# Attention quotients: one transfer for each head in place of one for a pair of heads

## The chip, the cores and the metric

The kernel runs on one core of one Trainium2 chip. The core has a matrix engine (TensorE, PE in the profile), a vector engine (VectorE, DVE), a scalar engine (ScalarE, ACT), a general engine (GpSimd, POOL) and SyncE (SP), which here only issues transfers; sixteen DMA engines move the data. The metric is the time of one execution on the device in microseconds (us), the median of several runs. Lower is better.

## The reference

Sixteen heads (2 batches of 8) of attention over 768 tokens with head dimension 64, where a query sees only the keys of its own cluster, and then two feed-forward parts over all 1536 tokens. The quotients of this case are the divisions by the softmax sums.

```python
mask = q_assign[:, :, :, None] == k_assign[:, :, None, :]
scores = np.where(mask, scale * np.matmul(q, k.transpose(0, 1, 3, 2)), -1e9)
scores = scores - np.max(scores, axis=-1, keepdims=True)
attn = np.exp(scores)
attn = attn / (np.sum(attn, axis=-1, keepdims=True) + 1e-09)
x = np.matmul(attn, v)                 # (2, 8, 768, 64)
x = x.transpose(0, 2, 1, 3).reshape(1536, 512)
x = ((x @ w1) * (x @ w2) @ w3) @ w_out # first feed-forward part
h = x @ w_in
out = softplus(h) @ w_out2             # second
```

## The kernel before

Attention is worked through in eight pairs of heads (`pi` 0 to 7). A pair has three blocks of 256 queries (`T`, 0 to 23 over all pairs), and a block has three slots (`o`, 0 to 71), one for each 256 keys. In a slot TensorE makes the scores (`st_pe`, L723, into the bank `sb`), ScalarE takes the exponential (`st_exp`, L730), and TensorE multiplies the slot before by V (`av_pe`, L741); after a block's third slot `sum_pe` (L751) sums the exponentials into the other half of the same bank `avb`. Every score is made of two matmuls: one over 128 rows of the operands, and one over 97 rows, whose last row is the row minimum of the block (the scores are held negated).

This minimum comes round a corner. `mx` (L671, L677) makes a block's scores ahead of time and VectorE reduces them to columns `mn`; `m_row` (L701 to L712) turns the columns into rows on TensorE (L705), ScalarE copies them to a tile `mr` (L65), and two small transfers `q<-mr` (L710, 1 KB each) put them on partition 96 of the query tile `q`. The second matmul of the block's first score reads that row.

The sums take another way, `r_ev` (L764 to L783) and `av_ev` (L756 to L762): to a DRAM buffer `sd` (L762), back as columns `r` (L771), one over the sum on VectorE (L774, L777), to a DRAM buffer `rd` of two rows of 768 numbers, one row for each head of the pair (L779), and from there to the tile `R` of 128 partitions (L783): row 0 copied to partitions 0 to 63, row 1 to partitions 64 to 127. `x_norm` (L793, GpSimd) multiplies the unscaled result by `R`.

The attention part is recorded with a fixed order: what stands first in the code stands first in its engine's queue, and each engine works its queue in order. The four steps of `r_ev` for a pair come at the ends of four slots in the first half of the next pair, the last of them being L783; the next slot begins with `m_row`, and so SyncE issues `q<-mr` right behind `R<-rd`. `x_norm` comes two slots later. Almost all transfers are issued by SyncE and go through one queue; they signal on eight semaphores in turn, so that each waits for the landing of the one eight places before it. Beside attention, TensorE works out a product of the weights w3 and w_out (L555, L574), whose weights come in loads of 512 KB (`w3r`, L93). For each next pair, SyncE loads heads (`rawqk`), and copies split queries and keys to the operand tiles (L360 to L367). After slot 72 the two feed-forward parts follow (L912, L934, L1213, L1282).

Of the kernel before, what the change touches and what calls it, by code (L numbers as in the profile page):

```python
# [27 lines left out]
def fused_kernel(ctx: ExitStack, tc, q, k, v, centroids, w1, w2, w3, wo, w_in, w_o2, out):  # L28
# [6 lines left out]
    nc = tc.nc  # L35
    B, H, S, D = q.shape
# [620 lines left out]
    MN, E, TT, R = {}, {}, {}, {}  # L657
# [106 lines left out]
    def r_ev(pi, i):  # L764

        if i == 0:
            pass
        elif i == 1:
            R["t", pi] = sp.tile([P, 8, QC], F32, tag="r", name=f"r{pi}")
            s = R.pop(("s", pi)).rearrange("r b n -> r (b n)")  # L770
            nc.sync.dma_start(R["t", pi][:, :4], s.rearrange("r (a x) -> a r x", x=QC))  # L771
        elif i == 2:
            t = R.pop(("t", pi))
            nc.vector.scalar_tensor_tensor(  # L774
                out=t[:, 4:6], in0=t[:, 0:4:2], scalar=1e-9, in1=t[:, 1:4:2], op0=ALU.add, op1=ALU.add
            )
            nc.vector.reciprocal(t[:, 6:], t[:, 4:6])  # L777
            R["d", pi] = drp.tile([2, S], F32, tag="rd", name=f"rd{pi}")
            nc.sync.dma_start(R["d", pi].rearrange("j (a x) -> a j x", x=QC), t[:, 6:])  # L779
        else:  # L780
            R[pi] = sp.tile([P, S], F32, tag="R", name=f"R{pi}", bufs=1)
            d = R.pop(("d", pi))
            nc.sync.dma_start(R[pi], d.unsqueeze(1).to_broadcast([2, D, S]))  # L783

    def x_norm(pi):
        b, c = divmod(pi, CC)
# [227 lines left out]
    with tc.manual_schedule():  # L1014
# [71 lines left out]
        for o in range(NSLOT + 1):  # L1086
# [48 lines left out]
            for pi in range(NPAIR):  # L1135
                r = a - 3 * NB * pi - 3 * NB
                if r in RS:
                    r_ev(pi, RS.index(r))
                if r == XR:
                    x_norm(pi)  # L1140
# [14 lines left out]
    for i in range(4):  # L1155
        r_ev(NPAIR - 1, i)
# [194 lines left out]
```

## Time and profile before

| what | value |
|---|---|
| median of 3 runs | 891.96 us (887.86 to 892.52) |
| the profiled execution | 889.03 us, its span 887.0 us |
| TensorE busy | 814.9 us, 92% of the span |
| VectorE, ScalarE, GpSimd busy | 439.3, 396.2 and 222.8 us |
| mean granted clock of TensorE | 0.96 |
| moved by DMA | 76.00 MB, mean 86 GB/s |

The profile is that of one execution. A wait is shown with the instruction that ended it. The chain is the work that ended last, followed back from the end: time on it is time that the kernel took, other work is beside it. A busy time of TensorE is a modelled one, since matmuls overlap. The granted clock is a share of 2.4 GHz: 1.00 is that, 0.50 is 1.2 GHz. A DMA share is the mean over sixteen engines.

### The profile page before, as it was taken

Reading aid. Unit: us, or ns where it says so; the run is one execution under the profiler, and the core shown is the slowest. Engines: PE = TensorE matmul, PEld = TensorE weight load, DVE = VectorE, ACT = ScalarE, POOL = GpSimd, SP = SyncE. Lnnn points to the kernel's source line nnn. Section 1 sums busy time; section 2 is a strip of 40 time slices with the busy share of each in tenths; the row PEclk is TensorE's granted clock in tenths of the full one; section 3 lists DMA queues with packets and bytes.
Section 4 is the critical chain, followed back from the end, with each engine's and each line's share of the span. In section 5 each row is a group of like instructions: output and inputs, shape, how many; then the busy total and the mean of one; then the engine's idle time right before and its main releaser. Section 6 shows DMA issues by size and latency. Waiting matters only on the chain.

```text
span 887.0 us, 11964 instructions
## 1 busy us (share of the span) xinstructions
PE 814.9 (92%) x4640; PEld 628.6 (71%) x4640; DVE 439.3 (50%) x736; ACT 396.2 (45%) x668; POOL 222.8 (25%) x204
## 2 busy tenths in 40 slices
PE   6988588897889998688999999999999999999997
PEld 5666366665657775455888888888877888888886
DVE  6667264253645656230533324434888844464443
ACT  3555243343534444243543334545554654455442
POOL 4323221202422120102340122231444322222221
PEclk9999699898989999898999999999999999999999
DMA  8846383462835317112630122341020010001001
GB/s 171 202 123 154 93 189 89 107 156 84 207 109 131 94 45 175 59 41 73 207 120 5 49 94 79 111 143 48 24 93 4 1 47 1 1 1 48 1 1 47
DMA packets 68336, 76.00 MB, mean 86 GB/s; under 512 B 35012, under 2 KB 53624, under 8 KB 68280
## 3 DMA queue, kind: packets, MB, share of 16 engines
q1 hardware_dynamic: 67208, 74.52, 31.3%
q8 instruction: 36, 0.59, 0.3%
q10 hardware_dynamic: 1072, 0.72, 0.3%
q14 instruction: 20, 0.16, 0.1%
HBM read 50.46 MB, written 3.29 MB: 61 GB/s over the span
## 4 chain that ended last, share of the span: by engine, by line
PE 72%; DVE 10%; DMA 9%; ACT 4%; issue 2%; POOL 1%; SPq 1%; ACTq 0%; POOLq 0%; DVEq 0%
DMA q<-mr 8%; PE sb L912 7%; PE rb L912 7%; PE sb L1213 6%; PE rb L1213 6%; PE avb L741 6%; PE mb L1282 6%; PE sb L723 6%; PE rb L574 4%; PE avb L751 4%; PE mb L934 4%; PE avb L1282 3%; PE rb L1282 3%; PE mb L671 3%; DVE mn L677 2%
## 5 line engine op out<-in xcount | busy, mean ns | idle before, releaser
L677 DVE TENSOR_REDUCE mn<-mb 128x1 f32<-128x768 f32 x94 | 89.6, 954 | 104.3 <-PE mb L671 103.7
L723 PE MATMUL sb<-q,k 128*128 128x256 f32 x576 | 92.0, 303 | 41.6 <-DMA q<-mr 41.0
L730 ACT ACTIVATE E<-sb 128x1024 f32<-128x1024 f32 x72 | 73.8, 1025 | 100.8 <-PE sb L723 100.3
L723 PEld LDWEIGHTS sb<-q,k 128*128 128x128 f32 x576 | 80.9, 202 | 46.0 <-DMA q<-mr 43.0
L78 POOL TENSOR_TENSOR u<-u,t 128x512 f32<-128x512 f32 x47 | 66.2, 1409 | 175.6 <-DVE u L1236 175.6
L741 PE MATMUL avb<-E,v 128*64 128x256 f32 x576 | 84.2, 416 | 0.3 <-ACT E L730 0.2
L1213 PE MATMUL sb<-ys,wh_i 128*128 128x512 f32 x192 | 65.2, 401 | 3.0 <-ACT t L1224 3.0
L671 PE MATMUL mb<-k,q 128*128 128x384 f32 x188 | 56.3, 381 | 11.7 <-DVE mn L677 4.9
L1213 PE MATMUL rb<-ys,wh_i 128*128 128x512 f32 x192 | 63.7, 394 | 0.0
L1226 DVE TENSOR_SCALAR u<-t 128x512 f32<-128x512 f32 x48 | 25.3, 527 | 74.0 <-ACT t L1225 74.0
L912 PE MATMUL sb<-xs,wh 128*128 128x512 f32 x192 | 61.5, 391 | 0.0
L912 PE MATMUL rb<-xs,wh 128*128 128x512 f32 x192 | 61.4, 391 | 0.0
L741 PEld LDWEIGHTS avb<-E,v 128*64 128x64 f32 x576 | 36.9, 144 | 25.9 <-issue 10.0
L78 POOL TENSOR_TENSOR wl_o<-d_o,wh_o 128x512 fp32r<-128x512 f32 x16 | 21.4, 1337 | 118.8 <-ACT wh_o L63 118.8
L671 PEld LDWEIGHTS mb<-k,q 128*128 128x128 f32 x188 | 29.1, 192 | 28.3 <-DVE mn L677 13.3
L1235 ACT ACTIVATE u<-u 128x512 f32<-128x512 f32 x48 | 30.4, 633 | 41.9 <-DVE t L1232 41.8
L81 DVE TENSOR_TENSOR gl<-u,gh 128x512 fp32r<-128x512 f32 x48 | 37.9, 789 | 15.8 <-ACT gh L63 15.2
L1213 PEld LDWEIGHTS sb<-ys,wh_i 128*128 128x128 f32 x192 | 36.6, 191 | 12.5 <-ACT t L1224 4.1
L793 POOL TENSOR_TENSOR xT<-t,R 128x256 f32<-128x256 f32 x24 | 17.4, 754 | 97.9 <-DMA R<-rd 77.4
L912 PEld LDWEIGHTS sb<-xs,wh 128*128 128x128 f32 x192 | 36.0, 188 | 8.2 <-issue 0.4
L1213 PEld LDWEIGHTS rb<-ys,wh_i 128*128 128x128 f32 x192 | 36.0, 188 | 8.1
L912 PEld LDWEIGHTS rb<-xs,wh 128*128 128x128 f32 x192 | 36.1, 188 | 7.8
(225 smaller groups left out, 1779.7 us busy)
## 6 DMA issues: line engine op xcount, KB each, us to landing
w3r<-in_moe_w_dram SPq DMA_DIRECT2D x16, 512.0 KB
w12r<-in_moe_w_dram SPq DMA_DIRECT2D x16, 512.0 KB
wir<-in_moe_w_in_dram SPq DMA_DIRECT2D x16, 512.0 KB
wor<-in_moe_w_out_dram SPq DMA_DIRECT2D x16, 512.0 KB
q<-H SPq DMA_DIRECT2D x16, 384.0 KB
w3r<-in_moe_w_out_dram SPq DMA_DIRECT2D x8, 512.0 KB
k<-H SPq DMA_DIRECT2D x16, 192.0 KB
v<-in_v_dram SPq DMA_DIRECT2D x16, 192.0 KB
```

Of the source, the lines that this page charges most:

```text
L78: nc.gpsimd.tensor_tensor(out=o, in0=i, in1=hi, op=ALU.subtract)
L81: return nc.vector.tensor_tensor(out=o, in0=i, in1=hi, op=ALU.subtract)
L574: nc.tensor.matmul(m, a[:, ks], bb, start=(mc == 0 and x == 0), stop=(mc == NK - 1 and x == 2))
L671: nc.tensor.matmul(bank[:, hf, :HALF], QT[pi][:, j, 0, c * P : (c + 1) * P], KT[pi][:, j, 0, hf * HALF : (hf + 1) * HALF], start=True, sto ...
L677: nc.vector.tensor_reduce(out=MN[pi][:, b, u : u + 1], in_=bank[:, :, :HALF], op=ALU.min, axis=AX.XY)
L723: nc.tensor.matmul(sbank[:, j, i * QB : (i + 1) * QB], KT[pi][: P - 31 * n, j, n, ks], QT[pi][: P - 31 * n, j, n, qs], start=(n == 0), sto ...
L730: nc.scalar.activation(E[o].rearrange("p j i q -> p j (i q)"), sbank, AF.Exp, scale=-1.0)
L741: nc.tensor.matmul(avbank[D * j : D * j + D, :QB], V[pi][:, j, 2 * kp + i, :], e[:, j, i, :], start=(kp == 0 and i == 0), stop=(kp == 2 an ...
L751: nc.tensor.matmul(avbank[32 * r : 32 * r + 32, QB:], ones[:, :32], e[:, r // 2, r % 2, :], start=(kp == 0), stop=(kp == 2),)
L912: nc.tensor.matmul(bk[:, :BLK], a[:, sl], bb, start=(n == 0), stop=(n == 3 * CC - 1))
L1213: nc.tensor.matmul(hbank[(bl * NF2 + fc) % 4][:, :BLK], a[:, sl], bb, start=(n == 0), stop=(n == 3 * CC - 1))
L1282: nc.tensor.matmul(ob, a[:, sl], bb, start=(fc == 0 and n == 0), stop=(fc == NF2 - 1 and n == 2),)
```

## The change

`R` is filled by two transfers in place of one: for each head, its row of `rd` is copied to 64 partitions.

```diff
             R[pi] = sp.tile([P, S], F32, tag="R", name=f"R{pi}", bufs=1)
             d = R.pop(("d", pi))
-            nc.sync.dma_start(R[pi], d.unsqueeze(1).to_broadcast([2, D, S]))
+            for j in range(2):
+                nc.sync.dma_start(R[pi][D * j : D * j + D], d[j : j + 1].to_broadcast([D, S]))
```

The source of the one transfer has three dimensions: 2 rows, 64 copies of each (step 0), 768 numbers. The source of each of the two has two: 64 copies (step 0) of one row, 768 numbers. Bytes and rows written stay the same: 128 rows of 3072 bytes. Lines after L783 move down by one.

In SyncE's queue, before, around the first pair's `R` (`rd` the quotients in DRAM, `mr` the minima of a block of the second pair, `v` the third pair's values, `w3r` weights):

```order
L779 DMA rd_941<-r_881 128x2x6
L762 DMA sd_945<-t_943 4x256
L93 DMA w3r_976<-in_moe_w_dram 128x1024
L783 DMA R_983<-rd_941 128x1x768
L710 DMA q_406<-mr_986 1x2x128 x2
L638 DMA v_1020<-in_v_dram 128x384 x2
```

The same place after the change:

```order
L779 DMA rd_941<-r_881 128x2x6
L762 DMA sd_945<-t_943 4x256
L93 DMA w3r_976<-in_moe_w_dram 128x1024
L784 DMA R_983<-rd_941 64x768 x2
L710 DMA q_406<-mr_987 1x2x128 x2
L638 DMA v_1021<-in_v_dram 128x384 x2
```

Nothing changes places; one more transfer stands ahead of `q<-mr`, in each of the eight pairs. On the other engines the order is the same through all of attention; one scaling of a weight on ScalarE stands two places later at the start of the feed-forward parts.

## Rows read from the trace of the kernel before

**Rows 1.** The page: chain that ended last, shares of the span by line.
```profile
DMA q<-mr 8%; PE sb L912 7%; PE rb L912 7%; PE sb L1213 6%; PE rb L1213 6%; PE avb L741 6%; PE mb L1282 6%; PE sb L723 6%; PE rb L574 4%; PE avb L751 4%; PE mb L934 4%; PE avb L1282 3%; PE rb L1282 3%; PE mb L671 3%; DVE mn L677 2%
```

**Rows 2.** TensorE's waits from 60 to 414 us: total us, times, longest.
```profile
PE sb L723 <- DMA q<-mr: 41.0, 8, 9.3
PE mb L671 <- DVE mn L677: 4.5, 8, 1.4
```

**Rows 3.** Timeline of SyncE: start, us, transfers issued; from 87 to 394 us.
```profile
87.94 0.59 SPq L783 DMA_DIRECT2D R<-rd  x1
88.62 1.24 SPq L710 DMA_DIRECT2D q<-mr  x2
...
146.52 1.47 SPq L710 DMA_DIRECT2D q<-mr  x2
...
205.18 1.21 SPq L710 DMA_DIRECT2D q<-mr  x2
...
255.24 1.23 SPq L710 DMA_DIRECT2D q<-mr  x2
...
302.54 0.57 SPq L783 DMA_DIRECT2D R<-rd  x1
311.04 1.22 SPq L710 DMA_DIRECT2D q<-mr  x2
...
354.42 1.24 SPq L710 DMA_DIRECT2D q<-mr  x2
...
393.43 1.19 SPq L710 DMA_DIRECT2D q<-mr  x2
```

**Rows 4.** Timeline of TensorE at scores' waits: idle before, with releaser, in brackets.
```profile
90.76 0.36 PE L723 MATMUL sb<-q,k 128*128 128x256 f32 x1
100.40 1.86 PE L723 MATMUL sb<-q,k 97*128 97x256 f32 x7 [9.28 <-DMA q<-mr]
...
133.12 1.11 PE L723 MATMUL sb<-q,k 97*128 97x256 f32 x7 [2.20 <-DMA q<-mr]
...
157.67 1.86 PE L723 MATMUL sb<-q,k 97*128 97x256 f32 x7 [5.54 <-DMA q<-mr]
...
215.94 1.86 PE L723 MATMUL sb<-q,k 97*128 97x256 f32 x7 [5.28 <-DMA q<-mr]
...
244.39 1.86 PE L723 MATMUL sb<-q,k 97*128 97x256 f32 x7 [3.77 <-DMA q<-mr]
...
264.49 1.10 PE L723 MATMUL sb<-q,k 97*128 97x256 f32 x7 [2.38 <-DMA q<-mr]
...
364.54 1.86 PE L723 MATMUL sb<-q,k 97*128 97x256 f32 x7 [6.53 <-DMA q<-mr]
...
401.57 1.86 PE L723 MATMUL sb<-q,k 97*128 97x256 f32 x7 [6.03 <-DMA q<-mr]
```

**Rows 5.** Stretches: us, each engine's busy us, granted clock, DMA share, GB/s.
```profile
97.00:99.00 2.00, 0.00 (x0) 0.00 (x0) 0.00 (x0) 0.00 (x0) 0.00 (x0) 0.50 0.13 49
154.00:156.00 2.00, 0.00 (x0) 0.00 (x0) 1.41 (x4) 0.45 (x2) 0.00 (x0) 0.66 0.13 49
126.00:128.00 2.00, 2.00 (x13) 1.28 (x13) 1.55 (x2) 0.94 (x2) 0.00 (x0) 1.00 1.03 270
267.00:350.00 83.00, 81.69 (x616) 60.02 (x608) 50.64 (x86) 38.81 (x62) 12.82 (x15) 1.00 0.47 116
```

**Rows 6.** Chain in order of time: the piece after L723, L741 and L751 of six waits.
```profile
106.89 0.55 PE mb L671 x2
...
162.89 0.55 PE mb L671 x2
...
221.09 0.55 PE mb L671 x2
...
268.04 2.99 PE rb L574 x12
...
370.42 0.55 PE mb L671 x2
...
407.70 1.17 PE sb L723 x8
```

**Rows 7.** Chain: a small transfer with nothing large ahead, issue to its reader.
```profile
79.75 3.00 DMA r<-sd
```

## The prediction

> **What bounds the kernel now.** I read the chain that ended last first, because only time on it can be won. It is nearly all TensorE, and its largest single entry is no matmul but the landing of a 1 KB transfer, `q<-mr`, with 8% of the span, some 71 us [rows 1]. Second, TensorE's waits in attention: 41.0 us of idle time in eight waits, all of L723 for `q<-mr`; the next reason, VectorE's minimum, is only 4.5 us [rows 2]. Third, SyncE's timeline, to see what stands ahead of that transfer: `R<-rd` at 87.94, `q<-mr` at 88.62 [rows 3]. TensorE issued its last matmul before the wait at 90.76 and went on at 100.40, idle for 9.28 us [rows 4]. So 2 KB took some 12 us.
>
> Fourth, what the DMA engines did meanwhile. From 97 to 99 us no engine of the core works at all, and the DMA share is 0.13 at 49 GB/s; 154 to 156 us reads the same [rows 5]. 0.13 of sixteen engines is two engines, 24.5 GB/s each. A busy stretch of the same queue shows share 1.03 and 270 GB/s [rows 5]. What was in flight is `R`: 128 x 3072 bytes = 393 KB, which at 49 GB/s takes 8.0 us. I read this as: `R` runs on two engines, `q<-mr` stands behind it on the same ones, and TensorE waits for both.
>
> Six of the eight waits come right after an `R`: 9.28, 5.54, 5.28, 2.38, 6.53 and 6.03 us, together 35.0. The other two, 2.20 at 133.12 and 3.77 at 244.39 [rows 4], come behind the large copies of L360 to L367 and stay. Of the eight pairs, the fifth doesn't wait, since its `q<-mr` is issued only at 311.04, 8.5 us after `R` at 302.54 [rows 3], when `R` is nearly through; the last has no block behind it.
>
> **The change part by part.** *The transfer itself.* 393 KB over all sixteen engines at 270 GB/s take 1.5 us; on two they take 8.0. I take 1.5. The bound on the other side is 8.0 us, no gain, for no row shows a transfer that reads one DRAM row from many engines.
>
> *One more issue.* The new issue costs SyncE 0.59 us and a gap of about 0.06 [rows 3], so `q<-mr` is issued 0.65 us later in each pair. Behind it stand the loads of `v` and `w3r`, which nobody waits for within a microsecond. Its wait for the transfer eight places ahead is met: those are small copies issued several microseconds before. As a pure cost, if TensorE still waited everywhere, it would be 6 x 0.65 = 3.9 us.
>
> *When does `q<-mr` land now?* The two take 1.24 us to issue, so the second starts 0.62 after the first [rows 3]; a small transfer that nothing large precedes needs 3.00 us from its issue to its reader [rows 7]. So the row is there at the old first issue + 0.65 + 0.62 + 3.00 = + 4.27 us. TensorE reaches the wait at its restart less the idle time [rows 4]:
> first pair: there at 92.9, wanted at 91.1: still 1.8 us of wait;
> second: 150.8 against 152.1; third: 209.4 against 210.7; fourth: 259.5 against 262.1: none;
> sixth: 358.7 against 358.0: 0.7; seventh: 397.7 against 395.5: 2.2.
> Won: 35.0 - 4.7 = **30.3 us**.
>
> *The clock.* After most of these waits TensorE goes on at granted clock 0.50, 1.2 GHz (0.50 from 97 to 99 [rows 5]). The same work, seven matmuls of L723, eight of L741 and 24 of L751, took 3.55 us after the shortest wait (264.49 to 268.04), whose L723 ran at the full 1.10 us, and 6.49, 5.22, 5.15, 5.88 and 6.13 us after the others, each from the restart [rows 4] to the next piece [rows 6]. The surplus is 2.94 + 1.67 + 1.60 + 2.33 + 2.58 = 11.1 us. In the second, third and sixth pair next to no wait is left: 5.6 us come back. In the first and the seventh about 2 us of wait stay; after 2.38 us the clock held, after 3.77 us L723 took the slow 1.86 [rows 4], so I take half of 5.5: 2.8. Together **8.4 us** (5.6 to 11.1).
>
> *What is late next.* During a wait VectorE works off a backlog: from 154 us, two microseconds after TensorE stopped, it still had 1.41 us of work [rows 5]. With no wait, TensorE has 3.55 us of its own before it needs a new minimum from VectorE, so the backlog is about covered. Without that cover it costs 1 to 3 us a pair. I take **2 us** in all, with 0 and 6 as bounds. Otherwise TensorE is the limit: from 267 to 350 us, without such waits but for short ones, it is busy 81.69 of 83 us and VectorE 50.64 [rows 5], so what is won isn't taken by another engine at once.
>
> *`R` itself and GpSimd.* `x_norm` gets `R` sooner, but it is not on the chain, and the last pair's is needed only well into the first feed-forward part. Nothing for it.
>
> Sum: 30.3 + 8.4 - 2 = 36.7 us. Against the profiled execution, 889.03 us with a span of 887.0 (the 2 us around it unchanged), 852.3; the median of the runs is 3 us higher, at 891.96, which would give 855. I say **853 us**.
>
> **What the skill says.** The rows show that the one transfer uses two engines' worth [rows 5]. The Trainium skill, page "DMA: Bandwidth & Descriptors", section "Rules for kernel authors", says of two transfers to disjoint partition halves not to bother, since both spray over the same sixteen engines and run one after the other. By that the sum would be only the added issues, 889.0 + 3.9 = 893. The trace doesn't bear out its premise here. The Trainium skill has, on the page "DMA: Bandwidth & Descriptors", section "Why a DMA increments its semaphore by 16 and not by 1", the number of engines as the largest up to 16 that divides the slowest dimension of both sides, which is 2 before and 16 after; with it the sum stands as it is, and no row of before shows a transfer with 64 zero-step copies outermost.
>
> **The rivals.** *Slower: each half on one engine.* If a source of one row, copied, is kept to one engine, the lowest, both halves run one after the other there: 2 x 196.6 KB at 24.5 GB/s = 16.0 us in place of 8.0. Each of the six waits grows by 8.0 + 0.65, 52 us in all, and the fifth pair, free now, waits some 6: about 945. It decides if the two together use fewer than two engines at a time. For it: no row shows such a source spread. Against it: that a source dimension of 2 gave two engines speaks for the outer count, 64, being what is split.
>
> *Engines many, speed the same.* Sixteen engines read one 3 KB row of DRAM, and could hold each other up. At an unchanged 49 GB/s nothing is won (893); if `R` ends 2.5 us earlier instead of 6.5, six waits give 15 us and no clock: 874. Against it: two engines already read one row each and keep 24.5 GB/s.
>
> *The wait moves to VectorE.* If the backlog costs 3 us in each of the six pairs, 16 more than I took are lost: 868. For it is the 1.41 us at 154 us; against it that VectorE is 61% busy where TensorE doesn't wait [rows 5].
>
> *Nothing happens.* The rule on partition halves holds after all, by whatever engines: 893.
>
> **How the numbers follow.** Forecast 0.78; wait moved to VectorE 0.06; engines many but slow 0.07, of which 0.06 on the faster side and 0.01 at no change; nothing 0.04; one engine each 0.05. The forecast's own range: all waits and all clock back, no backlog, 889.0 - 35.0 - 11.1 = 843; at the other end a microsecond more wait in three pairs (27), clock 5.6, backlog 6, from the median: 892 - 27 = 865. A part of the cases of VectorE and of the slow engines falls just above; with 867 as the upper end about two in ten are left out. A measurement of this kernel can tell about 0.5%, 4.5 us, from no change. Faster by over that: 0.78 + 0.06 + 0.06 = 0.90; within: 0.05; slower: 0.05.
>
> **What would show it.** In the profile after: the DMA share behind an `R` near 1 for 1 to 2 us in place of 0.13 for 8; L723's wait for `q<-mr` near 11 us in place of 41.0 [rows 2], with 2.20 and 3.77 still there; L723 x7 at about 1.1 us in the second, third and sixth pair; `q<-mr` on the chain at about 2 to 3% of the span. It would be wrong if the share stays at 0.13 or falls to 0.06, or if L671's waits for VectorE rise from 4.5 us [rows 2] to over 15.

## The result, and the profile after

The changed kernel takes 849.08 us (median of 4 runs, 847.16 to 851.12) against 892.24 for the kernel before beside it: a ratio of 0.953, with a 95% interval of 0.949 to 0.956. A second set of runs gave 846.43 us and 0.953 (0.950 to 0.956). It is 43 us faster; 853 was forecast, in a range of 843 to 867. The profiled execution took 847.16 us with a span of 845.3, against 889.03 and 887.0.

The page of the changed kernel, its engines and its chain by line:

```profile
PE 807.4 (96%) x4640; PEld 625.9 (74%) x4640; DVE 440.5 (52%) x736; ACT 396.2 (47%) x668; POOL 222.2 (26%) x204
...
PE sb L913 8%; PE rb L913 8%; PE avb L741 7%; PE sb L1214 6%; PE sb L723 6%; PE rb L1214 6%; PE mb L1283 6%; PE rb L574 5%; PE avb L751 4%; PE mb L935 4%; PE mb L671 4%; PE avb L1283 3%; PE rb L1283 3%; DVE mn L677 2%; DMA q<-mr 2%
```

`q<-mr` headed the chain with 8% [rows 1] and now ends the list with 2%. TensorE's waits in attention, from 60 to 376 us (us in total, times, longest):

```profile
PE sb L723 <- DMA q<-mr: 8.3, 4, 3.7
PE mb L671 <- DVE mn L677: 4.7, 7, 1.4
PE mb L671 <- DMA rd<-r: 2.9, 1, 2.9
PE sb L723 <- issue: 1.6, 1, 1.6
```

The wait for `q<-mr` fell from 41.0 to 8.3 us, that for VectorE's minimum stayed at 4.5 to 4.7 [rows 2]. The timeline of TensorE shows which waits are left (idle time and releaser in brackets):

```profile
94.07 1.22 PE L723 MATMUL sb<-q,k 97*128 97x256 f32 x7 [2.58 <-DMA q<-mr]
...
124.85 1.28 PE L723 MATMUL sb<-q,k 97*128 97x256 f32 x7 [1.67 <-DMA q<-mr]
...
209.06 1.08 PE L723 MATMUL sb<-q,k 97*128 97x256 f32 x7 [1.59 <-issue]
...
223.64 1.12 PE L723 MATMUL sb<-q,k 97*128 97x256 f32 x7 [3.73 <-DMA q<-mr]
```

Of the six waits behind an `R` [rows 4] only the first pair's is left, 2.58 of 9.28 us. The two behind the large copies are still there, 1.67 and 3.73 where 2.20 and 3.77 stood. One of 1.59 us is new; this profile names no releaser for it. And the transfer, in stretches of two microseconds (each engine's busy time, granted clock, DMA share, GB/s), behind the second pair's `R`, issued at 137.54:

```profile
138.00:140.00 2.00, 2.00 (x13) 1.18 (x13) 1.74 (x3) 1.58 (x2) 0.00 (x0) 1.00 0.80 299
140.00:142.00 2.00, 2.00 (x11) 1.60 (x10) 0.00 (x0) 0.00 (x0) 0.00 (x0) 1.00 0.84 233
```

`R` shares these with the loads issued around it, at shares of 0.80 and 0.84; before, it sat there alone at 0.13 [rows 5]. TensorE doesn't stop, and the clock stays at 1.00. The fifth pair's `R`, issued at 278.07 with no large transfer beside it, shows its own pace:

```profile
279.00:280.00 1.00, 1.00 (x7) 0.84 (x6) 0.30 (x1) 0.00 (x0) 0.29 (x1) 1.00 0.53 120
280.00:281.00 1.00, 1.00 (x11) 1.00 (x9) 1.00 (x2) 0.58 (x1) 0.00 (x0) 1.00 0.85 240
281.00:282.00 1.00, 1.00 (x11) 0.58 (x9) 1.00 (x3) 0.60 (x1) 0.00 (x0) 1.00 0.12 34
```

These three microseconds moved 394 KB, which is `R`; a share of 0.85 is the work of at least fourteen engines. GpSimd, which waits for the second pair's `R`, has it 5.3 us after its issue (its timeline):

```profile
142.81 2.12 POOL L794 TENSOR_TENSOR xT<-t,R 128x256 f32<-128x256 f32 x3 [8.68 <-DMA R<-rd]
```

In the kernel before it took 11.7 us (timelines of SyncE and of GpSimd):

```profile
145.84 0.58 SPq L783 DMA_DIRECT2D R<-rd  x1
```

```profile
157.50 2.11 POOL L793 TENSOR_TENSOR xT<-t,R 128x256 f32<-128x256 f32 x3 [13.90 <-DMA R<-rd]
```

The whole gain lies in attention. The chain in order of time, the first pair's restart, that behind the large copies, and the first matmuls of the feed-forward part:

```profile
94.07 1.22 PE sb L723 x7
95.29 1.91 PE avb L741 x8
97.19 1.99 PE avb L751 x24
99.18 0.55 PE mb L671 x2
...
228.77 0.59 PE rb L555 x4
...
372.98 5.79 PE sb L913 x24
```

The pieces that answer to the last two in the kernel before:

```profile
250.61 0.59 PE rb L555 x4
...
414.95 5.79 PE sb L912 x24
```

The feed-forward part begins 42.0 us earlier, and the spans differ by 41.7.

### The profile page after: what moved, and what is told of

Same layout as the page of the kernel before. It is cut to its first block, busy times and chain, and to the rows that moved or that the text cites. A ratio compares the mean times of both kernels' runs of the same rounds, so it can differ in the third digit from the quotient of the medians.

```text
span 845.3 us, 11985 instructions
## 1 busy us (share of the span) xinstructions
PE 807.4 (96%) x4640; PEld 625.9 (74%) x4640; DVE 440.5 (52%) x736; ACT 396.2 (47%) x668; POOL 222.2 (26%) x204
## 3 DMA queue, kind: packets, MB, share of 16 engines
q1 hardware_dynamic: 67448, 74.53, 32.7%
## 4 chain that ended last, share of the span: by engine, by line
PE 78%; DVE 9%; ACT 4%; DMA 3%; issue 2%; POOL 1%; SPq 1%; ACTq 0%; POOLq 0%; DVEq 0%
PE sb L913 8%; PE rb L913 8%; PE avb L741 7%; PE sb L1214 6%; PE sb L723 6%; PE rb L1214 6%; PE mb L1283 6%; PE rb L574 5%; PE avb L751 4%; PE mb L935 4%; PE mb L671 4%; PE avb L1283 3%; PE rb L1283 3%; DVE mn L677 2%; DMA q<-mr 2%
## 5 line engine op out<-in xcount | busy, mean ns | idle before, releaser
L723 PE MATMUL sb<-q,k 128*128 128x256 f32 x576 | 85.9, 291 | 10.4 <-DMA q<-mr 8.3
L723 PEld LDWEIGHTS sb<-q,k 128*128 128x128 f32 x576 | 76.1, 191 | 13.9 <-DMA q<-mr 9.1
L741 PE MATMUL avb<-E,v 128*64 128x256 f32 x576 | 81.6, 406 | 0.3 <-ACT E L730 0.2
L671 PE MATMUL mb<-k,q 128*128 128x384 f32 x188 | 56.4, 381 | 11.0 <-DVE mn L677 5.1
L741 PEld LDWEIGHTS avb<-E,v 128*64 128x64 f32 x576 | 36.1, 140 | 24.8 <-issue 8.1
L1236 ACT ACTIVATE u<-u 128x512 f32<-128x512 f32 x48 | 30.4, 633 | 41.8 <-DVE t L1233 41.6
L671 PEld LDWEIGHTS mb<-k,q 128*128 128x128 f32 x188 | 28.9, 191 | 27.7 <-DVE mn L677 13.4
L1214 PEld LDWEIGHTS sb<-ys,wh_i 128*128 128x128 f32 x192 | 36.7, 191 | 12.6 <-ACT t L1225 4.0
L1214 PE MATMUL sb<-ys,wl_i 128*128 128x512 f32 x96 | 38.1, 397 | 0.0
```

The source lines that it names most:

```text
L671: nc.tensor.matmul(bank[:, hf, :HALF], QT[pi][:, j, 0, c * P : (c + 1) * P], KT[pi][:, j, 0, hf * HALF : (hf + 1) * HALF], start=True, sto ...
L723: nc.tensor.matmul(sbank[:, j, i * QB : (i + 1) * QB], KT[pi][: P - 31 * n, j, n, ks], QT[pi][: P - 31 * n, j, n, qs], start=(n == 0), sto ...
L741: nc.tensor.matmul(avbank[D * j : D * j + D, :QB], V[pi][:, j, 2 * kp + i, :], e[:, j, i, :], start=(kp == 0 and i == 0), stop=(kp == 2 an ...
L1214: nc.tensor.matmul(hbank[(bl * NF2 + fc) % 4][:, :BLK], a[:, sl], bb, start=(n == 0), stop=(n == 3 * CC - 1))
```

## The experiments

All ratios are against the kernel before, run on the same chip: e1 to e4 on one, e5 to e8 on another, e9 to e11 on a third. TensorE's waits are those from 60 to 420 us.

**e1: the order alone.** The one transfer stays as it was, but is issued a slot later, behind `q<-mr`.

```diff
-    RS = 0, 1, 2, 3
+    RS = 0, 1, 2, 4
```

> The kernel before, its one transfer for R unchanged, but issued one slot later, behind the two q<-mr transfers in place of ahead of them (x_norm stays where it is). If q<-mr waits because it stands behind R on the same two DMA engines, it is enough to change the order: R still takes 8 us at a DMA share of 0.13, the six waits of L723 after an R (35.0 us) go, those behind the large copies (about 6 us) stay, and the time is 845 to 853 us. If a quick R itself is what the change brought (GpSimd's x_norm, or fewer bytes in flight beside other work), the time stays within 5 us of 892.

Measured: 867.77 us, ratio 0.975 (0.971 to 0.979). Neither number. TensorE's waits show why:

```profile
PE avb L741 <- ACT t L63: 18.6, 6, 5.9
...
PE sb L723 <- DMA q<-mr: 3.7, 4, 1.9
```

The wait for `q<-mr` is gone by the order alone, to 3.7 us, so it was the place behind `R` that held it. But a new wait stands in its place. The chain of this kernel in order of time, for the first pair's `R`:

```profile
94.37 10.82 DMA R<-rd
...
105.26 0.73 POOL xT L793
...
106.01 0.61 ACT t L63
...
106.66 1.97 PE avb L741 x8
```

The slow `R` comes a slot later, GpSimd's `x_norm` with it, and until that has read the tiles `t` ScalarE can't copy the next block's result out of the bank `avb`, which TensorE wants for the next block.

**e9: the order, and six tiles t in place of four.**

```diff
-        t = TT[T] = sp.tile([P, 2 * QB], F32, tag="t", name=f"t{T}", bufs=4)
+        t = TT[T] = sp.tile([P, 2 * QB], F32, tag="t", name=f"t{T}", bufs=6)
```

> As e1_order_only (the one slow transfer behind q<-mr), with six buffers in place of four for the tiles t, which hold the unscaled results until x_norm has R. In e1 the waits for q<-mr went, but TensorE then waited 18.6 us for ScalarE's copy into t, which waited for GpSimd's x_norm, which waited for R. If the lack of a free t is all that a late R costs there, this wait goes and the slow transfer does no harm: 841 to 849 us. If a late R holds something else too, 855 to 868.

Measured: 850.47 us, ratio 0.957 (0.954 to 0.960); a microsecond and a half over the first range, and 4.5 below the second. The wait on `t` is gone:

```profile
PE mb L671 <- DVE mn L677: 9.6, 10, 3.1
PE sb L723 <- DMA q<-mr: 4.8, 2, 3.3
```

So an `R` on two engines does little harm if nothing wanted soon stands behind it and enough tiles cover its delay: 4 us against the changed kernel on the same chip (e10, 846.43 us). What is left over is a wait for VectorE of 9.6 us in place of 4.5 [rows 2].

**e2: two engines again, by a cut.** Four transfers for each `R`: 62 and 2 partitions for each head.

```diff
-            nc.sync.dma_start(R[pi], d.unsqueeze(1).to_broadcast([2, D, S]))
+            for j in range(2):
+                for o, n in [(0, 62), (62, 2)]:
+                    nc.sync.dma_start(R[pi][D * j + o : D * j + o + n], d[j : j + 1].to_broadcast([n, S]))
```

> Each head's transfer of 64 partitions is cut into one of 62 and one of 2, so four transfers for each R. 62 has no divisor up to 16 but 2 (and 1). If the number of engines is set by a common divisor of the outer counts, 62 rows go over two engines as before, R takes 8 us again and q<-mr waits as before: DMA share 0.13, waits of L723 for q<-mr near 41 us, time 889 to 896 us with two more issues than after. If it is the cut into one transfer for each head that helps, whatever the number of engines, the time is 849 to 854.

Measured: 892.44 us, ratio 1.004 (1.001 to 1.006). TensorE's waits, and a stretch of the wait behind the seventh pair's `R`:

```profile
PE sb L723 <- DMA q<-mr: 40.8, 8, 9.7
```

```profile
398.00:400.00 2.00, 0.00 (x0) 0.00 (x0) 0.00 (x0) 0.00 (x0) 0.00 (x0) 0.50 0.13 49
```

The same 0.13 and 49 GB/s as in the kernel before, and the same waits. The cut by heads brings nothing in itself; the number of engines does.

**e3 and e11: four transfers again, of 48 and 16 rows,** both multiples of 16.

```diff
+                for o, n in [(0, 48), (48, 16)]:
```

> The control for the cut 62 and 2: each head's transfer cut into 48 and 16 partitions, both divisible by 16. Four issues for each R and all sixteen engines. Two issues more than in the changed kernel are 1.2 to 1.3 us more ahead of each q<-mr; where TensorE still waits (first pair) this shows fully, elsewhere it is hidden: 850 to 855 us. If the number of issues were what costs, 6 to 8 us more than 849.

> The four transfers of 48 and 16 partitions once more (e3). If the small shift of q<-mr against the other transfers is what leaves fewer waits and slow restarts, again 842 to 845 us, 4 to 6 below the changed kernel; if not, 846 to 852.

Measured: 843.61 us, ratio 0.948 (0.945 to 0.951), below the expected 850 to 855, and the second time 848.96 us, 0.955 (0.952 to 0.958). The 5 us below the changed kernel didn't come again; two more issues for each `R` cost nothing that can be measured, and gain nothing. e2 has as many issues and the same bytes, so what differs between them is the number of engines.

**e10: the changed kernel again, beside e11.**

> The changed kernel once more, beside e11 on one chip. If 849.08 us stands, 846 to 851. If the 5 us between it and e3 came from the chip or the hour, both lie within 2 us of each other.

846.43 us, 0.953 (0.950 to 0.956): the result stands, 2.5 us below e11. Between sets of runs one kernel moves by up to 5 us.

**e4: one engine.** The cut is 61 and 3.

> Each head's transfer cut into 61 and 3 partitions; 61 is prime. This is the price of the slower rival: if the outer count's divisor sets the engines, 61 rows sit on one engine, both heads' on the same one, R takes 16 us at a DMA share of 0.06 and each of six waits grows by 8 us against the kernel before: 935 to 950 us. If the rows of a transfer are dealt out in another way (a few rows less on some engines), 849 to 855.

Measured: 948.13 us, ratio 1.065 (1.061 to 1.070). TensorE's waits over the whole execution, for here attention runs to 466 us, and a stretch behind the sixth pair's `R`:

```profile
PE sb L723 <- DMA q<-mr: 87.7, 9, 17.6
```

```profile
406.00:408.00 2.00, 0.00 (x0) 0.00 (x0) 0.00 (x0) 0.00 (x0) 0.00 (x0) 0.50 0.06 25
```

One engine, 25 GB/s. This is the slower rival: it was priced at 945. The rows of `R` are the same in e2, e3 and e4, in four transfers each, and e2 and e4 are cut one row apart; two engines for 62 rows and one for 61 is what a divisor of the number of rows gives.

**e5: the clock.** The kernel before, with useless matmuls ahead of the five scores that wait and restart slowly.

```diff
+    WARM = {15: 135, 24: 80, 33: 76, 60: 95, 69: 86}
     def st_pe(o):
+        w = ones.bitcast(BF16)
+        for _ in range(WARM.get(o, 0)):
+            nc.tensor.matmul(sbank[:, 1, :P], w, w, start=True, stop=True)
```

> The kernel before with matmuls of no use ahead of the five scores that wait for q<-mr and restart at the low clock (135, 80, 76, 95 and 86 of 128x128, 60 ns each, into the scores' bank before the scores overwrite it). The waits stay, but TensorE works through most of them. If the 11.1 us of surplus after the restarts are the clock's, they come back: L723 x7 at about 1.1 us after each wait, the wait's start later, its end the same, time 878 to 883 us. If the surplus had another cause, 889 to 893.

Measured: 882.15 us against 889.57, ratio 0.992 (0.988 to 0.995). The first and the last of the five in the timeline of TensorE (L720 is the useless work):

```profile
92.27 7.70 PE L720 MATMUL sb<-ones 128*128 128x128 bf16 x135
...
102.64 1.71 PE L728 MATMUL sb<-q,k 97*128 97x256 f32 x7 [2.50 <-DMA q<-mr]
104.28 1.98 PE L746 MATMUL avb<-E,v 128*64 128x256 f32 x8
...
389.49 4.96 PE L720 MATMUL sb<-ones 128*128 128x128 bf16 x86 [0.16 <-ACT E L735]
...
396.26 1.11 PE L728 MATMUL sb<-q,k 97*128 97x256 f32 x7 [1.63 <-DMA q<-mr]
397.30 1.08 PE L746 MATMUL avb<-E,v 128*64 128x256 f32 x8
```

The data come no sooner, TensorE only doesn't rest, and four of the five restarts run at full speed (the last one's scores and the product with V behind them take 1.11 and 1.08 us; before, its scores took 1.86 [rows 4]); the first still slows after 2.50 us of idleness. So the surplus after a restart is the clock's: 7 us by the medians, 8.6 by the spans, of the 11.1 counted. The mean granted clock is 0.988, 0.964 before.

**e6: R on ScalarE's queue.**

```diff
-            nc.sync.dma_start(R[pi], d.unsqueeze(1).to_broadcast([2, D, S]))
+            nc.scalar.dma_start(R[pi], d.unsqueeze(1).to_broadcast([2, D, S]))
```

> The kernel before with its one transfer for R issued by ScalarE, on a queue of its own, at the same place. R keeps its shape, so its two engines and its 8 us. If q<-mr waited because one queue's work on an engine is done in order, it now takes turns with R's packets on those engines and lands within about 2 us: waits of L723 near 8 us, time 848 to 858, ScalarE paying 0.6 us for each of eight issues. If an engine holds all later work until a transfer is through, whichever queue it came from, 888 to 895.

Measured: 862.66 us, ratio 0.971 (0.968 to 0.975), between the two.

```profile
PE sb L723 <- DMA q<-mr: 22.1, 9, 4.9
```

The wait about halves, so the order in one queue is one part of it. The rest stays though `R` is in another queue; that it comes from the two engines that both use is likely but not shown, and how the two queues take turns wasn't found out.

**e7: the change and the order together.** The changed kernel with the edit of e1.

> The changed kernel (two transfers for R) issued one slot later, behind q<-mr. q<-mr is issued 1.2 us earlier and nothing of R is ahead of it: the first pair's wait of 2.58 us and its slow restart (1.6 us) go or shrink: 845 to 849 us. If what is left in that wait is the weights' load ahead of it, 848 to 850.

Measured: 841.99 us, ratio 0.947 (0.944 to 0.949): below the range. The first pair's wait is gone as expected:

```profile
PE sb L723 <- DMA q<-mr: 4.8, 2, 3.2
```

Its interval ends where the changed kernel's two (0.949 and 0.950) begin. It is the fastest kernel here together with e8. That it beats the changed kernel by some 5 us isn't shown: the two were not run beside each other, and a kernel moved by as much between sets (e3, e11).

**e8: also one of three q<-mr on ScalarE's queue,** that behind the large copies.

```diff
+        q_ = nc.scalar if b == 1 else nc.sync
         for j in range(2):
-            nc.sync.dma_start(
+            q_.dma_start(
```

> As e7, and the q<-mr of each pair's second block, which stands behind the large copies of L360 to L367, is issued by ScalarE on its own queue. If the order in the queue is what holds it, the two waits left (1.67 and 3.73 us) and their slow restarts (3 us) go, at 1.2 us of ScalarE for each of six blocks: 838 to 845 us. If ScalarE's issues cost the exponentials time, 848 to 855.

Measured: 841.59 us, ratio 0.947 (0.944 to 0.950): in the expected range, but no gain over e7.

```profile
PE mb L671 <- DVE mn L677: 8.7, 10, 2.0
PE rb L705 <- DVE mn L677: 3.8, 3, 2.3
...
PE sb L724 <- DMA q<-mr: 1.2, 2, 0.9
```

The waits for `q<-mr` fall from 4.8 to 1.2 us, those for VectorE's `mn` rise from 6.0 in e7 (5.1 at L671, 0.9 at L705) to 12.5. Here, with nearly all transfers out of the way, the wait does move to VectorE.

## Why the prediction was right

*The reading.* `R` on two engines, `q<-mr` behind it on the same ones, TensorE behind both: e2 and e4 show the first (two engines 892, one 948, the change 849 us, with the same bytes), e1 the second (with the order turned, the waits for `q<-mr` go though `R` is no quicker).

*The transfer.* Taken at 1.5 us against 8.0. The fifth pair's `R`, alone, moves its bytes within 3 us, most of them in one, so it is nearer to the 1.5.

*One more issue.* Forecast were 0.65 us. `q<-mr` is issued 1.23 us behind `R` in the first pair, 0.68 before [rows 3]: 0.55 us, as SyncE's timeline shows:

```profile
88.30 1.14 SPq L784 DMA_DIRECT2D R<-rd  x2
89.53 1.29 SPq L710 DMA_DIRECT2D q<-mr  x2
```

*Waits left.* 4.7 us were forecast for the six (1.8, 0.7 and 2.2 in the first, sixth and seventh pair), 2.58 were measured, all in the first. The term that was mis-sized is the landing of `q<-mr`, taken at 3.00 us from a transfer with another shape [rows 7]. In the seventh pair the two are issued from 360.32 us, and the scores that need them start at 362.06 and run through, as the timelines of SyncE and TensorE show:

```profile
360.32 1.29 SPq L710 DMA_DIRECT2D q<-mr  x2
```

```profile
362.06 1.23 PE L723 MATMUL sb<-q,k 128*128 128x256 f32 x8 [0.16 <-ACT E L730]
```

The last of these scores needs both heads' rows, so both were there within 3 us of the first issue, not 3.62. In the first pair it took 4.5 us from the issue at 89.53 to the restart. There `R` itself and, ahead of it, a weights load of 512 KB (L93) precede the small transfers, and the step's 3.00 us come from one with nothing large ahead. The load alone isn't the cause: in e7 it still stands ahead, only `R` doesn't, and the block's scores start 2.8 us after the issue and run through (timelines of SyncE and TensorE):

```profile
87.68 1.26 SPq L710 DMA_DIRECT2D q<-mr  x2
```

```profile
90.50 1.25 PE L723 MATMUL sb<-q,k 128*128 128x256 f32 x8
```

One number for both was wrong on both sides. With the two waits that stay and 0.28 us elsewhere, L723's waits for `q<-mr` are 8.3 us; 32.7 were won, 30.3 forecast.

*A wait not foreseen.* 1.6 us at 209.06, where the kernel before didn't stop. In e3 and e11 the profile puts the wait at this place down to `q<-mr` (3.31 us at 207.72, 1.51 at 209.91). It belongs to the next pair's first block, issued at 205.91 right behind a weights load, and not to one behind an `R`.

*The clock.* 8.4 us forecast. The seven, eight and 24 matmuls after the first pair's wait take 94.07 to 99.18, 1.56 us over 3.55; the other four surpluses are gone: 11.12 - 1.56 = 9.6 won. One restart behind the large copies, at 223.64, is shorter too, 5.13 in place of 6.22 us: 1.1 more. e5 shows that it is the clock.

*The backlog.* 2 us were taken off for VectorE; next to nothing was lost, TensorE's waits for it are 4.7 in place of 4.5 us.

*The sum.* 32.7 - 1.6 + 9.6 + 1.1 = 41.8 us; the spans differ by 41.7. Forecast were 36.7. The mechanism held; the 5 us are what was won of the waits (32.7 for 30.3), the clock (10.7 for 8.4) and the backlog (2.0), less the new wait.

*The rivals.* One engine: not the case here. Its price, 945, came out where it is (948 in e4), but in part by luck: it was made of 58 us of waits for `q<-mr`, and they grew by 46.7 (from 41.0 to 87.7). The feed-forward part begins 51.6 us later in e4, and the span is 59.2 us longer, so 7.6 us fell behind attention, where the price had nothing. Many engines but no faster: the 240 GB/s of the fifth pair's `R` say no, and GpSimd's 5.3 us where it was 11.7. The rule of the Trainium skill, page "DMA: Bandwidth & Descriptors", section "Rules for kernel authors", that two transfers to partition halves are not worth it, gives as its reason that both halves go over the same sixteen engines. Here the one transfer used two, so the reason didn't apply; where all are in use already, e3 and e11 agree with it (cut in four, nothing gained). The Trainium skill's rule for the number of engines, page "DMA: Bandwidth & Descriptors", section "Why a DMA increments its semaphore by 16 and not by 1", agrees with the cuts: 62 on two (0.13), 61 on one (0.06), 64 on at least fourteen (0.85). For 48 with 16 no run shows `R` alone; the time is that of 64.

*What the prediction missed.* It put nothing on a late `R` ("not on the chain"). That held for the change: neither before nor after does TensorE wait for a copy into `t`. But there was little room: in e1 the same `R`, issued one slot later, cost 18.6 us through the tiles `t`.

## What to carry to other kernels

A DMA share that stands still at a small multiple of one sixteenth, here 0.13 and 0.06, points to a transfer on so few engines: look at the outermost counts of its two sides. Here a multiple of 16 on both, at the cost of an issue, was enough. Ask first what stands behind the slow transfer in its queue: where order and buffers allow, moving it back won nearly as much here as making it quick (39 us in e9, 43 in e10). And a wait of TensorE costs more than its length where the clock falls: here 35.0 us of waits had 11.1 us of slow restarts behind them.

## What the runs showed of the hardware

A cut of 64 rows into 61 and 3, in place of 48 and 16, made the same kernel 12% slower, by the number of engines alone (948.13 and 843.61 us). SyncE's issues took longer, too: the four of the first pair's `R` 8.26 us in e4 (timeline of SyncE), against 1.77 in e3 and 1.53 in e2. Why was not found out. First e4, then e3:

```profile
89.88 8.26 SPq L785 DMA_DIRECT2D R<-rd  x4
98.23 1.27 SPq L710 DMA_DIRECT2D q<-mr  x2
```

```profile
87.46 1.77 SPq L785 DMA_DIRECT2D R<-rd  x4
```

And a queue of its own doesn't set a small transfer wholly free of a slow one: in e6 22.1 us of waits for `q<-mr` stayed of 41.0.
